# Block-sparse attention and an MLP-mixer on one Trainium2 core: the first head pair cut into row halves, a shorter gate, and a new instruction order

## The chip, the core and the metric

The kernel runs on one core of a Trainium2 chip. The core has five engines with their own in-order instruction queues: TensorE (PE in the profile; PEld is its weight load), VectorE (DVE), ScalarE (ACT), GpSimd (POOL) and SyncE (SP, which here only issues DMAs). The metric is device microseconds of one launch. The median of three runs of the kernel before is 264.33 us (264.31 to 272.79).

## What is computed

Inputs are q, k and v of shape (4, 8, 768, 64) and four MLP weights. Attention is by blocks of 64 keys: each query attends to its own block and to the three blocks with the highest gate score, all under the causal mask. A mixer follows, which mixes tokens and then channels.

```python
k_rep = k.reshape(B, H, n_blocks, block, D).mean(axis=3)
gate_scores = np.einsum('bhsd,bhnd->bhsn', q, k_rep)
gate_scores = np.where(causal, gate_scores, -1000000000.0)
top_idx = np.argsort(gate_scores, axis=-1)[..., -top_k:]
...
sel = set(top_idx[b, h, i].tolist()) | {own_block[i]}
...
scores = scale * np.matmul(q, k.transpose(0, 1, 3, 2))
mask = mask & (pos[:, None] >= pos[None, :])
attn = softmax(np.where(mask, scores, -1000000000.0))
x = np.matmul(attn, v)                          # (B, S, 512) for the mixer
...
h = np.maximum(xt @ w_tok1, 0.0) @ w_tok2
u = x + h.transpose(0, 2, 1)
h2 = np.maximum(u @ w_ch1, 0.0) @ w_ch2
return (u + h2).astype(np.float32)
```

(The softmax is written out in the reference; it is cut to one line here.)

## The kernel before

**Units of work.** The heads are taken in pairs: 4 batches of 4 pairs, 16 in all, and the 64 channels of the two heads of a pair lie on the two halves of the 128 partitions. `pair(p)` (from line 461) does one pair; `mlp(b)` (from line 693) does the channel MLP of one batch, which needs all four of its pairs.

**One pair.** k, q and v are loaded in fp32 (lines 470 to 478). For the first eight pairs ("early") k is turned by fp32 transposes on TensorE (line 486), summed over blocks of 64 by DVE (line 487), and copied to fp16 in `KA` by four copies (line 496). Later pairs have k cast to fp16 by GpSimd first (line 502), turned by six fp16 transposes (line 508) and copied by two copies (line 512); their block sums come from a separate computation per batch. q is turned in fp32 (line 519) and copied to `QT` (522), and to fp16 in `QA` (533). Twelve rows under the 64 channels of `QA` and `KA` carry the block mask: `KA` has a block indicator (`ind`, copied in line 379 ahead of everything else), `QA` a number per query and block, so that the matmul of the scores adds the mask by itself.

**The gate.** Pairs below `th` (pairs 0 to 3) use ten fp32 matmuls (line 543) of `QT` with block sums that are zero outside their own head (`ks2b`, spread by a product with `side`, line 491). The other early pairs split q and the sums into three bf16 parts (lines 499, 526, 552) and use fifteen bf16 matmuls (line 559) and three additions (564). After the causal bias (546), DVE takes the eight largest of the twelve scores (573), copies the third to PSUM (575), compares (576) and multiplies with `own`, which is 0 at a query's own block and -1 elsewhere (579). The result is turned, by TensorE (598) for pairs 0 to 4 and by DVE (584) and four small DMAs (587) from pair 5 on, and lands in `QA`.

**Scores, values, tokens.** Per head the 21 causal 128x128 tiles of scores go through three groups (`GROUPS`, line 18) of up to 1024 columns: matmuls (619), one exponential per group on ACT (626), a triangular mask on GpSimd for the diagonal tiles (634). Then 21 matmuls with v (643), the normalisation (646, 650), the token MLP (661, 665, 675, 678) and a transpose of its result (686). The channel MLP has 24 steps of four matmuls (704) with a ReLU (710, 712), and per output tile of 128 rows twelve matmuls of 512 columns (721), one addition (724) and one DMA (727).

**What sets the order.** Nothing is issued in program order. Each step is registered with `P.op(cost, function, reads, writes, priority)`. A planner (`Plan.run`, from line 114) then plays the queues forward with the given costs and picks on each engine, among what could start soon, the step with the lowest priority number. It chooses the engine too where a step names several. Priorities are the pair's time `T(p)`, set by `EARLY` and `PACE` (line 46), plus or minus a lead from the table `L` (line 47). `th` and `bd` in that table pick the kind of gate and of turning. Where TensorE would wait, matmuls of zeros are put in (line 766) until the first step of the channel MLP.

Of the kernel before, what the change touches and what calls it, by code (L numbers as in the profile page):

```python
# [17 lines left out]
GROUPS = [  # L18
# [3 lines left out]
]  # L22


def _layout():
    col, diag, width = {}, [], []
    for g, banks in enumerate(GROUPS):
        mine, w = [], 0
        for bk, pieces in enumerate(banks):
            at = 512 * bk  # L30
            for kk, q0, n in pieces:
                for i in range(n):
                    col[kk, q0 + i] = 1024 * g + at + 128 * i
# [4 lines left out]
        diag.append(mine)  # L38
        width.append(w)
    return col, diag, width  # L40


COL, DIAG, WIDTH = _layout()

EARLYP = 8
EARLY, PACE = 5.58, 13.33
L = dict(kd=28.57, qd=25.92, vd=11.57, va=-8.52, kt=12.35, kr=17.84, ke=-10.79, qt=15.5, qe=4.07, q16=14.86, g=19.74,
         b=14.78, k16=23.05, kx=14.61, kc=15.1, r=24.94, kb=35.09, ks=47.26, w1=2.86, w2=-1.57, wc1=17.92, wc2=28.28,
         tok=9.0, ml=12.54, o0=-0.3, o1=1.07, o2=2.31, o3=0.96, o4=-4.5, o5=1.61, o6=-2.0, o7=-4.89, o8=-4.68,
         o9=0.71, o10=0.86, o11=-1.11, o12=-2.65, o13=-2.86, o14=1.45, o15=0.65, m0=-2.18, m1=-0.36, m2=-0.52,  # L50
         m3=-1.94, th=3.11, bd=4.29)
# [207 lines left out]
def kernel(  # L259
# [84 lines left out]
    own1 = np.where(nidx[None, None, :] == mrow, 0.0, -1.0)  # L344
    both = np.stack([np.concatenate([a, a], axis=2)[:, 1:] for a in (gb1, own1)], axis=1).astype(np.float32)
# [8 lines left out]
    gbias, own = cst[:, 0], cst[:, 1]  # L354
# [3 lines left out]
    nc.gpsimd.memset(ind, MASKV)  # L358
# [3 lines left out]
    side = sb([128, 2, 6], FP, "side")  # L362
    nc.gpsimd.memset(side, 0.0)
    for x in range(2):
        nc.gpsimd.memset(side[64 * x:64 * x + 64, x], 1.0)
# [95 lines left out]
    def pair(p):  # L461
# [4 lines left out]
        early, thirds = p < FIRST, p >= L["th"]  # L466
        q32, k32, v32 = Buf(q32r), Buf(k32r), Buf(v32r)
        qs, ks_, vs = q[b, h:h + 2], k[b, h:h + 2], v[b, h:h + 2]
        QA, KA, VA, QT = Buf(QAr), Buf(KAr), Buf(VAr), Buf(QTr)
        for t, src, e, lead in ((k32, ks_, "SP", "kd"), (q32, qs, "ACT" if p == 0 else "SP", "qd")):  # L470
            for x in range(2):
                P.op({e: (500.0, 1600.0, 768 * 17.6 / 16)}, lambda x=x, t=t, src=src, e=e: ENG[e].dma_start(
                    out=t.t[:, :, x, :], in_=src[x].rearrange("(j p) d -> p j d", p=128)), wr=[(t, x)], pr=t0 - L[lead] - (99.0 if p == 0 else 0.0))
# [7 lines left out]
        if early:  # L481
            ks2b = kp = Buf(kppr if thirds else ksr)
            ks3 = Buf(ks3r) if thirds else None
            for i in range(2):
                t = Buf(Rr)
                P.op(pe(slow=3), lambda t=t, i=i: transposed(k32, i, t.t), rd=[(k32, 0), (k32, 1)], wr=[(t, 0)], pr=t0 - L["kt"])
                P.op(dve(HS), lambda t=t, i=i: nc.vector.tensor_reduce(
                    out=ks3.t[:, 0, 6 * i:6 * i + 6] if thirds else t.t[:, HS:HS + 6], in_=t.t[:, 0:HS].rearrange("c (n w) -> c n w", w=64),
                    axis=AX.X, op=ALU.add), rd=[(t, 0)], wr=[(ks3, i) if thirds else (t, 1)], pr=t0 - L["kr"])
                if not thirds:  # L490
                    P.op({"DVE": (150.0, 220.0)}, lambda t=t, i=i: nc.vector.tensor_tensor(
                        out=ks2b.t[:, :, 6 * i:6 * i + 6], in0=t.t[:, HS:HS + 6].rearrange("c (o n) -> c o n", o=1).broadcast_to([128, 2, 6]),
                        in1=side, op=ALU.mult), rd=[(t, 1)], wr=[(ks2b, i)], pr=t0 - L["kr"] + 0.1)
                for x in range(2):
                    def kev(e, t=t, i=i, x=x):
                        copy(ENG[e], KA.t[0:64, x, halves(i)], t.t[64 * x:64 * x + 64, 0:HS])
                    P.op({**dve(HS), **act(HS)}, kev, rd=[(t, 0)], wr=[(KA, (x, i))], pr=t0 - L["ke"])
# [312 lines left out]
```

## Time and profile before

| | |
|---|---|
| median of the runs | 264.33 us (264.31 to 272.79) |
| the profiled execution, its own time | 264.49 us |
| its span, first to last instruction | 262.8 us |
| mean granted TensorE clock | 0.998 |
| PE, DVE, ACT, POOL busy | 250.4, 157.3, 167.1, 120.0 us |
| first transposes of k / first scores / last addition start | 6.41 / 15.79 / 259.08 us |

All views show one execution. A row of the timeline or of a group names the line of the kernel, the engine, the operation and "out<-in" with the tiles' names (numbers left out), then partitions x elements and types. "x10" counts instructions. In brackets or behind the last bar stands the idle time of the engine before it, and who ended it. A busy PE is not a PE at its peak: matmuls are pipelined, and the time of one includes its latency.

### The profile page before, as it was taken

To read this page: it belongs to the slowest core of one execution; us is meant where nothing else is said; L and a number is where in the kernel's file an instruction comes from. 1 tells how busy PE (TensorE), PEld (TensorE's weight loads), DVE (VectorE), ACT (ScalarE), POOL (GpSimd) and SP (SyncE) were. 2 spreads that over 40 slices of the span, in tenths; PEclk is the share of its full clock that TensorE was granted. 3 is DMA by queue.
4 is the path that set the end of the run, shared out by engine and by line. 5 is a ranking of instruction groups with operands and counts; after the bars stand their busy time and mean duration, and the time that the engine had idled before them with its cause. 6 is when DMAs were issued, how large, how long until landed. Compare 5 with 4: busy or idle time off the path is not lost.

```text
span 262.8 us, 6757 instructions
## 1 busy us (share of the span) xinstructions
PE 250.4 (95%) x2585; PEld 172.1 (65%) x2585; DVE 157.3 (60%) x527; ACT 167.1 (64%) x265; POOL 120.0 (46%) x222
## 2 busy tenths in 40 slices
PE   7689999988999999999999999999999999999994
PEld 7566688775667677666776677657665665554541
DVE  5788997998368475786684767638574452301103
ACT  2689989975776683459974968457765661360520
POOL 8136884963256898666993807133132110000000
PEclk9999999999999999999999999999999999999999
DMA  8999997689998799943997940021002100212103
GB/s 165 224 211 215 231 221 148 102 139 146 179 269 139 190 246 220 241 85 126 213 219 158 216 114 2 8 80 42 7 2 75 54 0 2 80 40 80 44 0 120
DMA packets 88960, 33.21 MB, mean 126 GB/s; under 512 B 82464, under 2 KB 85152, under 8 KB 88736
## 3 DMA queue, kind: packets, MB, share of 16 engines
q1 hardware_dynamic: 83984, 28.33, 50.0%
q0 software_dynamic: 3232, 3.93, 9.8%
q10 hardware_dynamic: 1712, 0.52, 1.0%
q8 instruction: 20, 0.33, 0.5%
q14 instruction: 12, 0.10, 0.1%
HBM read 30.01 MB, written 6.29 MB: 138 GB/s over the span
## 4 chain that ended last, share of the span: by engine, by line
PE 83%; DVE 6%; DMA 4%; ACT 2%; issue 2%; SPq 1%; DVEq 0%; ACTq 0%
PE pm L704 20%; PE pm L721 18%; PE sc L619 12%; PE pm L643 7%; PE sc L721 5%; PE pm L419 4%; PE pm L661 4%; PE pm L675 3%; PE sc L704 3%; PE pm L559 2%; DMA k<-in_k_dram 2%; DMA QA<-bnt 2%; PE pm L686 2%; ACT E L626 1%; PE pm L508 1%
## 5 line engine op out<-in xcount | busy, mean ns | idle before, releaser
L626 ACT ACTIVATE E<-sc 128x1024 f16<-128x1024 f32 (+1 forms) x96 | 83.7, 918 | 13.8 <-PE sc L619 12.7
L634 POOL TENSOR_SCALAR_AFFINE_SELECT E<-E 128x256 f16<-128x256 f16 x96 | 38.8, 409 | 69.1 <-ACT E L626 68.6
L704 PE MATMUL pm<-uT,wc 128*128 128x384 f16 x340 | 64.3, 326 | 0.0
L721 PE MATMUL pm<-wc,h 128*128 128x512 f16 x228 | 59.2, 379 | 0.0
L704 PEld LDWEIGHTS <-wc 128*128 128x128 f16 x384 | 36.2, 98 | 23.2 <-issue 0.6
L619 PE MATMUL sc<-QA,KA 76*128 76x512 f16 (+3 forms) x256 | 49.0, 305 | 2.0 <-DMA QA<-bnt 1.1
L710 ACT ACTIVATE h<-pm 128x384 f16<-128x384 f32 x60 | 29.5, 492 | 20.9 <-PE pm L704 20.7
L721 PEld LDWEIGHTS <-h 128*128 128x128 f16 x288 | 26.6, 98 | 23.3 <-issue 1.0
L619 PEld LDWEIGHTS <-KA 76*128 76x128 f16 x256 | 22.8, 98 | 16.7 <-issue 2.9
L643 PEld LDWEIGHTS <-E 128*128 128x128 f16 x672 | 25.1, 98 | 4.9 <-issue 1.1
L643 PE MATMUL pm<-VA,E 128*128 128x65 f16 x651 | 25.5, 193 | 1.0 <-ACT uT L301 0.9
L724 DVE TENSOR_TENSOR os<-u,pm 128x512 f32<-128x512 f16 x19 | 12.9, 681 | 20.5 <-PE pm L721 19.1
L712 DVE TENSOR_SCALAR h<-pm 128x384 f16<-128x384 f32 x25 | 13.9, 555 | 13.1 <-PE pm L704 12.7
L449 POOL TENSOR_TENSOR kb<-kb 96x512 f32<-96x512 f32 (+2 forms) x18 | 20.0, 1114 | 0.0
L303 POOL CAST QA<-QT 64x768 f16<-64x768 f32 x12 | 9.8, 819 | 20.7 <-ACT QT L301 18.7
L724 DVE TENSOR_TENSOR os<-u,sc 128x512 f32<-128x512 f16 x5 | 3.3, 686 | 26.0 <-PE sc L721 26.0
L650 DVE TENSOR_TENSOR x<-pm,rc 128x384 f16<-128x384 f32 x31 | 17.2, 556 | 0.8
L678 DVE TENSOR_TENSOR u<-x,pm 128x384 f16<-128x384 f16 x30 | 15.5, 547 | 2.7 <-PE pm L675 2.5
L301 ACT COPY uT<-pm 128x384 f16<-128x384 f16 x21 | 9.1, 486 | 12.5 <-PE pm L686 12.5
L301 ACT COPY QT<-pm 128x384 f32<-128x384 f32 x24 | 11.0, 485 | 8.0 <-PE pm L419 7.8
L552 POOL TENSOR_TENSOR R<-R 128x640 bf16<-128x640 f32 x12 | 15.0, 1252 | 1.9 <-DVE R L526 0.9
L419 PE MATMUL pm<-id,q 128*128 128x128 f32 x96 | 14.6, 276 | 1.0 <-ACT QT L301 1.0
(90 smaller groups left out, 358.0 us busy)
## 6 DMA issues: line engine op xcount, KB each, us to landing
k<-in_k_dram SPq DMA_DIRECT2D x32, 192.0 KB
v<-in_v_dram SPq DMA_DIRECT2D x16, 384.0 KB
out_dram<-os SPq DMA_DIRECT2D x24, 256.0 KB
q<-in_q_dram SPq DMA_DIRECT2D x30, 192.0 KB
wc<-in_moe_w_ch_dram POOLq DMA_DIRECT2D x8, 384.0 KB, 6.3
kb<-in_k_dram SPq DMA_DIRECT2D x2, 1536.0 KB
w<-in_moe_w_tok_dram POOLq DMA_DIRECT2D x2, 384.0 KB, 6.2
QA<-bnt SPq DMA_DIRECT2D x44, 9.0 KB
```

Of the source, the lines that this page charges most:

```text
L301: e.copy(out=out, in_=in_)
L419: nc.tensor.transpose(out=t[:, 128 * j:128 * j + 128], in_=src.t[:, 3 * i + j].rearrange("p x d -> p (x d)"), identity=id32)
L449: P.op({"POOL": (step * 2.15 + 60, step * 2.15 + 140)}, lambda n=n, o=o, step=step: nc.gpsimd.tensor_tensor(out=kb.t[:, o:o + step] if n > ...
L619: nc.tensor.matmul(out=s.t[:, at:at + 128 * m], lhsT=KA.t[:, x, 128 * kk:128 * kk + 128], rhs=QA.t[:, q0:q0 + m, x, :], start=True, stop=True)
L626: nc.scalar.activation(out=E.t[:, 1024 * g_:1024 * g_ + WIDTH[g_]], in_=s.t[:, 0:WIDTH[g_]], func=AF.Exp, scale=scale)
L634: nc.gpsimd.affine_select(out=o, in_=o, pattern=[[0, 2], [1, 128]], compare_op=ALU.is_ge, fill=0.0, base=0, channel_multiplier=-1)
L643: nc.tensor.matmul(out=t[:, jq, :], lhsT=E.t[:, cc:cc + 128], rhs=VA.t[:, x, kk, :], start=(kk == 0), stop=(kk == jq))
L650: P.op(dve(384), lambda a=a, rc=rc, x=x: nc.vector.tensor_tensor(out=xp.t[:, :, 64 * x:64 * x + 64], in0=a.t[:, 0:NJ * 65].rearrange("p (j ...
L704: nc.tensor.matmul(out=m.t[:, 0:HS], lhsT=wc1[:, c, 128 * f:128 * f + 128], rhs=uT.t[:, c, HS * i:HS * i + HS], start=(c == 0), stop=(c == ...
L710: nc.scalar.activation(out=h2.t[:, f, :], in_=m.t[:, 0:HS], func=AF.Relu)
L721: nc.tensor.matmul(out=m.t, lhsT=h2.t[:, f, 128 * jj:128 * jj + 128], rhs=wc2[:, f, :], start=(f == 0), stop=(f == NFC - 1))
L724: P.op(dve(DM), lambda j=j, m=m, o=o: nc.vector.tensor_tensor(out=o.t.rearrange("p (c d) -> p c d", d=128), in0=u.t[:, :, j, :], in1=m.t.r ...
```

## The change

It has several parts, which the planner then orders anew.

1. **Pair 0 in row halves** (`CUT = 1`): its k and q come in row halves, with priorities that put the first halves first; transposes, sums, copies, gate, comparison and turning follow per half. The gate of the first half covers two of the five row tiles and six of the twelve blocks. A second layout of the score tiles, `HALVED`, puts the six tiles that need only the first halves into its first group. GpSimd may no longer make pair 0's fp16 q.
2. **Gate.** For fp32 gates the comparison reads the scores in PSUM and the third value directly; for all, it writes the mask, and two memsets on 64 partitions (GpSimd or DVE) clear each query's own block. The product with `own` is gone, and the indicator has its sign turned. Block sums always go to SBUF, and for fp32 gates two GpSimd copies spread them over the heads.
3. **k in fp16** for pairs 2 and 3 (`k0` to `k1`): GpSimd casts k, six fp16 transposes turn it, two copies fill `KA`. The fp32 transposes remain for the block sums.
4. **The last output tile** is made in two halves of 256 columns, each with its own matmuls, addition and DMA.
5. **New numbers** for nearly all priorities. `th` goes from 3.11 to 5.9, so that pairs 4 and 5 take the fp32 gate; `bd` (4.29 to 4.76) still means pair 5.

The diff, cut to its core:

```diff
+HALVED = [
+    [[(0, 1, 2), (0, 0, 1), (1, 1, 1)], [(2, 2, 1), (1, 2, 1)]],
+    [[(0, 3, 3), (5, 5, 1)], [(4, 4, 2), (1, 3, 2)]],
+    [[(2, 3, 3), (1, 5, 1)], [(3, 3, 3)]],
+]
...
-EARLY, PACE = 5.58, 13.33
-L = dict(kd=28.57, qd=25.92, vd=11.57, va=-8.52, kt=12.35, kr=17.84, ke=-10.79, qt=15.5, qe=4.07, q16=14.86, g=19.74,
...
-         m3=-1.94, th=3.11, bd=4.29)
+CUT = 1
+EARLY, PACE = 5.58, 14.57
+L = dict(kd=27.6, qd=26.51, vd=11.57, va=-8.12, kt=9.92, kr=21.45, ke=-10.79, qt=17.89, qe=-4.61, q16=15.3, g=19.76,
...
+         m2=4.07, m3=-2.96, th=5.9, bd=4.76, cu=-2.34, cs=0.51, k0=1.5, k1=3.5)
...
-    nc.gpsimd.memset(ind, MASKV)
+    nc.gpsimd.memset(ind, -MASKV)
...
-    side = sb([128, 2, 6], FP, "side")
-    nc.gpsimd.memset(side, 0.0)
-    for x in range(2):
-        nc.gpsimd.memset(side[64 * x:64 * x + 64, x], 1.0)
+    for t in ks2:
+        nc.gpsimd.memset(t, 0.0)
...
+        cut = p < CUT
+        dual = early and L["k0"] <= p < L["k1"] and not cut
+        GROUPS, COL, DIAG, WIDTH, BASE = LAYOUTS[cut]
+        parts = [(0, 2), (2, NJ - 1)] if cut else [(0, NJ - 1)]
...
+                for i in range(1 + cut):
+                    n = NJ // (1 + cut)
...
+                        out=t.t[:, n * i:n * i + n, x, :], in_=src[x, 128 * n * i:128 * n * i + 128 * n].rearrange("(j p) d -> p j d", p=128)),
+                        wr=[(t, (x, i) if cut else x)], pr=t0 - L[lead] - (99.0 - 0.2 * i if p == 0 else 0.0))
...
-                    P.op({"DVE": (150.0, 220.0)}, lambda t=t, i=i: nc.vector.tensor_tensor(
-                        out=ks2b.t[:, :, 6 * i:6 * i + 6], in0=t.t[:, HS:HS + 6].rearrange("c (o n) -> c o n", o=1).broadcast_to([128, 2, 6]),
-                        in1=side, op=ALU.mult), rd=[(t, 1)], wr=[(ks2b, i)], pr=t0 - L["kr"] + 0.1)
+                if not thirds and (cut or i == 1):
+                    def spread(z=slice(6 * i, 6 * i + 6) if cut else slice(0, NB)):
+                        for x in range(2):
+                            nc.gpsimd.tensor_copy(out=ks2b.t[64 * x:64 * x + 64, x, z], in_=ks3.t[64 * x:64 * x + 64, 0, z])
+                    P.op({"POOL": (210.0, 280.0)}, spread, rd=[(ks3, i)] if cut else [(ks3, 0), (ks3, 1)],
+                         wr=[(ks2b, i)] if cut else [(ks2b, 0), (ks2b, 1)], pr=at(i, L["kr"]) + 0.1)
+                if dual:
+                    continue
...
-        else:
+        if dual or not early:
             k16 = Buf(k16r)
...
-        P.op({"DVE": (140.0, 210.0)}, lambda: nc.vector.tensor_copy(out=third(), in_=m8.t[:, :, :, 2:3]), rd=[(m8, 0)], wr=[(g, 1)], pr=t0 - L["g"] + 0.25)
...
-            out=bn.t[:, 1:, :, 0:NB], in0=below(), in1=own.rearrange("p j (x n) -> p j x n", n=NB), op=ALU.mult),
...
+            def less(z0=z0, z1=z1, nb=nb, pair_of=pair_of):
+                u_, w_ = pair_of()
+                nc.vector.tensor_tensor(out=bn.t[:, 1 + z0:1 + z1, :, 0:nb], in0=u_, in1=w_.broadcast_to([128, z1 - z0, 2, nb]), op=ALU.is_lt)
...
+            def mine(e, z0=z0, z1=z1):
                 for x in range(2):
+                    o = bn.t[64 * x:64 * x + 64, 1 + z0:2 + z0, :, 0:1]
+                    o = bass.AP(tensor=o.tensor, offset=o.offset + 2 * (1 + z0) + x, ap=[o.ap[0], [66, z1 - z0], [32, 2]])
+                    ENG[e].memset(o, 0.0)
+            P.op({"POOL": (200.0, 270.0), "DVE": (140.0, 210.0)}, mine, rd=[(bn, i)], wr=[(bn, i)], pr=at(i, L["g"]) + 0.4)
...
+                wide = DM // 2 if b == B - 1 and j == NJ - 1 else DM
+                for w in range(0, DM, wide):
```

More of the change, by code (lines that the diff above doesn't have):

```diff
@@ L353 @@
     cstc = nc.inline_tensor(both, name="cstc").ap()
-    gbias, own = cst[:, 0], cst[:, 1]
+    gbias = cst
     nc.vector.memset(zero, 0.0)
@@ L582, in pair @@
+        bn_all = [(bn, i) for i in range(len(parts))]
         if p >= L["bd"]:
@@ L636, in pair @@
+                P.op({"POOL": (195.0 * len(DIAG[g_]), 195.0 * len(DIAG[g_]) + 50.0)}, mask, rd=[(E, g_)], wr=[(E, g_)], pr=tg + 0.2)
             a = Buf(Rr)
```

185 lines of the change are left out of this document (107 added, 78 removed).

## The prediction

> **What bounds the kernel now.** I read the page first, then the table of busy time by stretches, then the first 20 us in order of time, then the groups of instructions inside the stretch that the first two pointed to.
>
> ```profile
> span 262.8 us, 6757 instructions
> PE 250.4 (95%) x2585; PEld 172.1 (65%) x2585; DVE 157.3 (60%) x527; ACT 167.1 (64%) x265; POOL 120.0 (46%) x222
> PE   7689999988999999999999999999999999999994
> PEclk9999999999999999999999999999999999999999
> ```
>
> Over the whole span the matmul engine looks like the only bound, at full clock. The average hides two stages. The stretches (from:to, length, then busy us of each engine) part them:
>
> ```profile
> 0.00:6.40 6.40, 4.72 (x47) 4.58 (x48) 3.69 (x11) 1.49 (x2) 5.44 (x20) 1.00 0.82 162
> 6.40:15.80 9.40, 7.17 (x70) 6.46 (x71) 6.86 (x29) 6.92 (x14) 1.96 (x5) 1.00 1.20 212
> 15.80:59.00 43.20, 40.06 (x565) 32.30 (x565) 39.12 (x149) 39.41 (x59) 29.88 (x58) 1.00 1.00 181
> 59.00:64.30 5.30, 4.24 (x42) 2.67 (x41) 4.66 (x21) 2.78 (x6) 2.42 (x7) 1.00 0.98 133
> 64.30:100.00 35.70, 35.67 (x343) 23.95 (x344) 20.89 (x56) 25.93 (x39) 23.28 (x39) 1.00 0.99 205
> 100.00:150.00 50.00, 50.00 (x570) 34.66 (x569) 34.56 (x122) 33.62 (x52) 36.99 (x60) 1.00 0.89 182
> 150.00:200.00 50.00, 50.00 (x547) 34.52 (x545) 32.62 (x115) 33.95 (x54) 16.79 (x30) 1.00 0.16 45
> 200.00:259.00 59.00, 58.56 (x410) 32.91 (x408) 14.23 (x27) 23.02 (x43) 3.25 (x8) 1.00 0.12 43
> ```
>
> From 64.3 to 259 PE is busy 194.2 of 194.7 us while DVE and ACT idle a third of the time or more: there only PE work counts, and freed DVE time is worth nothing. Before 64.3 PE is idle 2.2 + 3.1 + 1.1 = 6.4 us (behind the first data), and DVE (39.12 of 43.2) and ACT (39.41) are both 91% busy between 15.8 and 59. No MLP work exists there until the first batch's four head pairs are through, so their evictions, gates and exponentials set the pace. Whatever brings that point forward brings the dense PE stretch, and the end, forward by as much, less any PE work added. The start in order of time (start, duration):
>
> ```profile
> 3.85 2.68 DVE L379 COPY KA<-ind 12x768 f16<-12x768 f16 x6 [1.72 <-POOL ind L360]
> 6.41 0.84 PE L419 MATMUL pm<-id,k 128*128 128x128 f32 x6 [0.61 <-DMA k<-in_k_dram]
> 6.96 0.96 ACT L301 CAST KA<-pm 64x384 f16<-64x384 f32 x2 [2.87 <-PE pm L419]
> 7.29 0.57 DVE L487 TENSOR_REDUCE pm<-pm 128x6 f32<-128x384 f32 x1 [0.76 <-PE pm L419]
> 15.79 0.59 PE L619 MATMUL sc<-QA,KA 76*128 76x512 f16 x3
> GB/s 0 0 0 0 0 0 0 0 0 0 0 0 81 203 213 174 133 195 210 249 285 283 293 285 285 291 286 275 221 218 221 211 224 220 217 228 227 223 248 238
> ```
>
> The data of pair 0 lands at about 6.3, and 9.4 us pass before the first scores at 15.79. The last row is the DMA rate in 40 parts of the first 6.3 us (0.1575 us each).
>
> **The change, step by step.** The profiled run took 264.49 us (span 262.8 plus 1.7 around it); the median is 264.33, so it stands 0.16 high. Terms are taken from 264.49.
>
> *(a) First loads in halves.* The same 2 x 393 KB of k and q are cut into row halves, first halves issued first on SP and on ACT. By the rate row 393 KB have moved by about 3.6 us and 786 KB by about 5.4; the data was usable at 6.3, so 0.9 after its last byte. The first halves are then usable at 4.5, 1.8 us sooner, and ACT's first eviction moves from 6.96 to some 5.1. DVE gains less: six copies of the block indicators (L379) stand ahead in its queue until 6.53, because GpSimd builds their source, and neither is changed. Its first reduction moves from 7.29 to 6.55. That is 1.85 + 0.75 = 2.6 us of two engines, 1.3 us of time. Ends: 0 (halves land together, shared with pair 1's loads) and 1.3; I take 1.1, near the upper, since issue order favours the first halves. More issues on SP (four for k instead of two, about 0.6 each by 2.56 us for four) delay pair 1's loads by 1.3 us; they were not what the engines waited for, so nothing is charged.
>
> [...]
>
> *(b) Work taken off DVE and ACT.* Groups inside 0 to 64.3 us (for the fp16 copies of k, later ones); behind the bar busy us, then mean ns. The last row gives shortest, median and longest in ns:
>
> ```profile
> L491 DVE TENSOR_TENSOR ks<-pm,side 128x12 f32<-128x12 f32 x8 | 1.2, 161 | 0.3 <-ACT KA L301 0.3
> L575 DVE COPY pm<-m 128x10 f32<-128x10 f32 x7 | 1.2, 175 | 0.0
> L579 DVE TENSOR_TENSOR bn<-pm,cst 128x120 f16<-128x120 f32 x6 | 1.7, 277 | 0.2 <-DVE rc L646 0.2
> L526 DVE TENSOR_TENSOR R<-pm,QT 128x256 f32<-128x256 f32 x3 | 1.2, 414 | 0.0
> L526 DVE TENSOR_TENSOR R<-pm,QT 128x384 f32<-128x384 f32 x3 | 1.6, 540 | 0.0
> L564 DVE TENSOR_TENSOR gm<-pm,gm 128x120 f32<-128x120 f32 x6 | 1.7, 281 | 0.1
> L303 DVE CAST KA<-pm 64x384 f16<-64x384 f32 x14 | 7.7, 552 | 0.3
> L301 ACT CAST KA<-pm 64x384 f16<-64x384 f32 x14 | 6.6, 474 | 5.1 <-PE pm L419 4.1 <-DVE KA L303 0.4 <-DVE pm L487 0.4
> L303 DVE COPY KA<-pm 64x768 f16<-64x768 f16 x11 | 6.1, 550 | 2.9 <-ACT E L626 2.1 <-PE pm L508 0.7
> L301 ACT COPY KA<-pm 64x768 f16<-64x768 f16 x5 | 4.0, 793 | 0.4 <-DVE KA L303 0.4
> L301 ACT CAST QA<-QT 64x768 f16<-64x768 f32 x7 | 5.8, 834 | 0.2
> L436 POOL COPY kpp<-ks 64x36 bf16<-64x36 bf16 x6 | 1.3, 209 | 0.3
> L365 POOL MEMSET side<- 64x6 f32 x2 | 0.5, 273 | 0.1
> L502 POOL CAST k<-k 128x768 f16<-128x768 f32 x8 | 6.5, 824 | 0.2
> L478 POOL CAST VA<-v x16: 817/826/840, 18.4 to 173.4; 128x768 f16<-128x768 f32 x16
> ```
>
> The block sums of pairs 0 to 3 are spread by two GpSimd copies instead of eight DVE multiplies: 8 x 0.161 = 1.3 off DVE. The product with `own` goes for every pair, 6 x 0.277 = 1.7 by this point. One line of the table of constants matters more than its size: `th` goes from 3.11 to 5.9, so pairs 4 and 5 leave the three-part bf16 gate for the fp32 one. With it go two subtractions each, 2 x (0.414 + 0.540) = 1.9, and two additions each, 4 x 0.281 = 1.1. The copy of the third score goes for the six pairs 0 to 5: 6 x 0.175 = 1.05. In pairs 2 and 3 eight evictions of k at a mean of 0.51 (4.1) become four of fp16, three on DVE and one on ACT as later pairs share them: 3 x 0.550 + 0.793 = 2.45, so 1.65 less. Against it pair 0 in halves pays more starts: GpSimd may no longer make its fp16 q (one copy there, one of 0.834 on ACT, become four of some 0.48 by the 64x384 row): +1.1; smaller pieces of gate and mask: an estimate of +0.6. The clears of own blocks go to GpSimd where it is free, else to DVE: +0.5. Sum 1.3 + 1.7 + 1.9 + 1.1 + 1.05 + 1.65 - 2.2 = 6.5 us of two engines, 3.2 us of time. Ends: 0, if PE or a chain of waits sets the pace, and 3.5; I take 3.2, because both engines are at 91%.
>
> GpSimd takes two copies per pair (the 64x36 row, 0.42 for both, as against 0.32 on DVE), two clears of small tiles (nearest the 64x6 memset, 0.27 each) and two casts of k (0.82 each), and loses pair 4's and 5's remainder and split. It is at 29.88 of 43.2, so this lies beside other work; what it costs if that cover is gone is the third rival.
>
> *(c) The first chain.* Two of five row tiles of the gate, then six of 21 score tiles, need only the first halves. From a reduction at 6.55: 0.57, the spread 0.42, two fifths of the fp32 gate's 1.03 below, and some 2 us (an estimate) for bias, maxima, comparison, clear, transposes and evictions; first scores near 10 instead of 15.79. In 6.4 to 15.8 DVE idles 2.5 us and ACT 2.5; exponentials that come earlier fill some of it. Ends 0 and 2.5 us of time; I take 1.2, midway, as nothing here shows the refill.
>
> *(d) PE work added.* Rows of the chain:
>
> ```profile
> 20.40 1.03 PE pm L543 x10
> 162.22 0.49 PE pm L559 x15
> 182.47 0.34 PE pm L508 x6
> ```
>
> Two fp32 gates for bf16 ones: 2 x 0.54 = 1.1. Fp16 transposes of k besides the fp32 ones, which the block sums still need: 2 x 0.34 = 0.7. Together 1.8, in the stage where PE idles 6.4 us plus fillers; but the stage also gets shorter. Ends 0 and 1.8; I take 0.9.
>
> *New order.* After 64.3 it can win no more than the 0.5 us that PE idles there to 259. What it could lose has no row; the nearest are the 6.4 us of idle PE before. MLP work is ready throughout, so I take 0.
>
> *(e) The last tile in two halves of columns.*
>
> ```profile
> 259.08 0.69 DVE L724 TENSOR_TENSOR os<-u,pm 128x512 f32<-128x512 f16 x1 [1.30 <-issue]
> GB/s 0 0 0 0 0 0 0 0 0 0 0 0 0 0 0 137 389 378 368 389 410 347 273 0 0 0 0 0 63 336 389 410 147 0 0 0 0 0 0 0
> ```
>
> The addition behind the last matmul falls from 0.69 to 0.41 (the 128x256 row above); the last transfer, five parts of 0.195 us here, halves: 0.45. Gain 0.3 to 0.7; I take 0.7. Nothing is queued behind it.
>
> Sum: 264.49 - 1.1 - 3.2 - 1.2 + 0.9 - 0.7 = 259.2 (about 259.0 for the median).
>
> **Rivals.** *Second: the freed time does not arrive.* PE is in order, and between 15.8 and 59 it shows 40.06 of 43.2, fuller than the other two. If the 1.8 us of PE work counts whole and (b) gives only a third: 264.49 - 1.1 - 1.1 - 1.2 + 1.8 - 0.7 = 262.2. That the halves land together (the change not doing what it says) gives 259.2 + 1.1 + 1.2 = 261.5 and belongs here. Against it: a pipelined matmul's latency counts as busy, so PE's real slack is larger than 3.1 us.
>
> *Third, slower: GpSimd's queue.* Spread and clear put two crossings of GpSimd into each gate, in a queue that sits on the diagonal masks, which wait for exponentials.
>
> ```profile
> POOL E L634 <- ACT E L626: 10.5, 13, 2.9
> ```
>
> That is 15 to 59 us: 13 waits, 0.81 each. Should each of the ten steps of pairs 1 to 5 stand behind one, and the lead of a pair not cover it, the gates lose 8.1 us: 264.49 - 5.3 + 8.1 = 267.3. It decides from 0.53 us a step (5.3/10). Against it: pairs are prepared ahead, and the first idle time behind a late gate is PE's, which had 3.1 us in all.
>
> [...]
>
> *Fourth: everything arrives.* (a) 1.3, (b) 3.5, (c) 2.5, (d) 0, (e) 0.7: 256.5. PE's visible slack allows it.
>
> **How the numbers follow.** First 0.48 (259.2; by itself 257.5 to 261.3), second 0.20 (262.2), third 0.14 (267.3, spread from 264.5 to 271), fourth 0.18 (256.5). The range 255.6 to 266.5 leaves out the upper half of the third and a little of the fourth, about 1 in 10 besides what was not thought of. A measurement of this kernel can tell about 2% from no change, 5.3 us: under 259.0 lie the fourth and less than half of the first, 0.39; over 269.6 a third of the third, 0.04; within, 0.57.
>
> **What would show it.** First k transposes near 4.5 to 5 us; DVE's first reduction at 6.55, right behind L379; first scores near 10. DVE's multiplies with `side` and `own` gone; two fp32 gates more. PE dense from about 59 instead of 64.3, with no idle behind it. The tail from the last matmul 0.7 shorter. The prediction is wrong if DVE or ACT falls clearly below 90% in 15 to 55 us while PE waits (second), if gates wait for GpSimd's spread or clear (third), or if PE idles after 65 us, since no term allows for the new order opening a gap there.

## The result and the profile after

The changed kernel takes 267.79 us (median of six runs, 266.29 to 269.14); the kernel before took 264.18 beside it. The ratio is 1.0138, with a 95% interval of 1.0102 to 1.0174: 3.6 us slower, where 5.3 faster was forecast. Runs of one kernel differ by the granted clock: none of the six of after had more than 0.994, while 61 of the 93 runs of before beside the experiments had 0.997 or more, so comparisons below name the clock where it matters.

The profiled run of after took 266.92 us. Its page:

```profile
span 264.9 us, 6889 instructions
PE 255.2 (96%) x2642; PEld 179.1 (68%) x2642; DVE 150.9 (57%) x513; ACT 169.3 (64%) x266; POOL 121.6 (46%) x240
PE   7799999999999999999999999999999999999993
PEclk9799999999999999999999999999999999999999
```

Over the whole span DVE lost 6.4 us of work, ACT gained 2.2 and PE 4.8, of which 2.7 are matmuls of zeros ahead of the first MLP step (8.9 us for 6.2). The clock row has a 7 in its second slice. Term (b) counts DVE and ACT up to about the first MLP step: there DVE fell from 49.68 to 46.50 us and ACT from 47.83 to 46.62, 4.4 us of two engines for the 6.5 forecast. The stretches, with the columns of the table in the prediction:

```profile
6.40:15.80 9.40, 7.52 (x78) 7.31 (x79) 5.29 (x25) 5.37 (x12) 0.96 (x6) 0.82 1.34 222
15.80:59.00 43.20, 41.99 (x588) 36.07 (x586) 36.02 (x130) 37.61 (x54) 29.11 (x67) 1.00 0.97 167
59.00:64.30 5.30, 5.19 (x49) 3.65 (x48) 3.96 (x10) 3.98 (x8) 3.59 (x7) 1.00 1.18 200
64.30:100.00 35.70, 35.70 (x359) 24.08 (x358) 21.02 (x70) 25.28 (x38) 23.38 (x39) 1.00 0.95 190
100.00:150.00 50.00, 49.45 (x548) 33.55 (x546) 33.96 (x123) 33.85 (x52) 37.99 (x62) 1.00 0.96 196
150.00:200.00 50.00, 50.00 (x565) 35.08 (x564) 32.05 (x119) 36.40 (x58) 18.34 (x32) 1.00 0.15 39
```

In 15.8 to 59 DVE fell from 39.12 to 36.02 and ACT from 39.41 to 37.61, while PE rose from 40.06 to 41.99. PE is dense from 59 on, as the prediction's list had it, and idles 0.55 us in 100 to 150, where before had none. Now the start of after in order of time:

```profile
3.86 2.96 DVE L383 COPY KA<-ind 12x768 f16<-12x768 f16 x6 [1.72 <-POOL ind L366]
4.39 0.87 PE L423 MATMUL pm<-id,k 128*128 128x128 f32 x3
4.54 0.41 ACTq L494 DMA_DIRECT2D cst<-cstc  x1
6.85 0.56 DVE L505 TENSOR_REDUCE ks<-pm 128x6 f32<-128x384 f32 x1
7.56 0.43 POOL L511 COPY ks<-ks 64x6 f32<-64x6 f32 x2 [1.77 <-DVE ks L505]
8.04 0.61 PE L576 MATMUL pm<-ks,QT 128*128 128x12 f32 x4 [2.11 <-POOL ks L511]
9.76 2.71 PE L829 MATMUL pm<-zero 128*128 128x120 f16 x28
12.65 0.75 PE L576 MATMUL pm<-ks,QT 128*128 128x24 f32 x6
13.43 0.32 DVE L580 TENSOR_TENSOR gm<-pm,cst 128x72 f32<-128x72 f32 x2 [2.32 <-PE pm L576]
16.42 0.49 PE L671 MATMUL sc<-QA,KA 76*128 76x256 f16 x5 [0.37 <-DVE QA L310]
```

The first halves are usable at 4.39 at the latest: zeros keep PE busy until about then, and it shows no wait for them. Then the lead is lost in three places. DVE holds the six indicator copies until 6.82, so the reduction runs at 6.85 and PE idles 2.11 us before the gate at 8.04. PE's queue has the next pair's transposes and 28 zeros ahead of the second half's gate (12.65). In DVE's queue both halves' bias additions stand together (x2 at 13.43), the second half's first, so the first half, whose gate was done at 8.65, waits for the second; the bias cst that they add is issued at 4.54, behind q's four transfers. The first scores come at 16.42, later than before. And the clock halves behind the idle 2.11 us (last columns: granted clock, DMA share, GB/s):

```profile
8.00:9.00 1.00, 0.96 (x7) 0.96 (x8) 0.44 (x1) 0.00 (x0) 0.00 (x0) 0.80 1.35 221
9.00:10.00 1.00, 1.00 (x8) 0.94 (x7) 0.00 (x0) 0.62 (x2) 0.00 (x0) 0.50 1.35 218
11.00:12.00 1.00, 1.00 (x13) 1.00 (x12) 0.11 (x1) 0.70 (x2) 0.37 (x2) 0.50 1.35 218
12.00:13.00 1.00, 1.00 (x15) 1.00 (x14) 0.00 (x0) 0.15 (x1) 0.00 (x0) 0.99 1.35 218
```

That is some 3.4 us at half speed (0.4 of the first row, then three whole ones). The tail:

```profile
258.96 0.49 PE L781 MATMUL sc<-wc,h 128*128 128x256 f16 x3 [0.51 <-DVE os L785]
261.46 0.41 DVE L785 TENSOR_TENSOR os<-u,sc 128x256 f32<-128x256 f16 x1
```

From the last matmul's end to the span's end it is 3.49 us (261.41 to 264.9) against 3.81 (258.99 to 262.8), but PE waited 0.51 just before.

The milestones of the profiled runs (us; "MLP" is the first step of the channel MLP):

| kernel | first k transposes | first scores | MLP | last matmul ends | span | clock |
|---|---|---|---|---|---|---|
| before | 6.41 | 15.79 | 59.01 | 258.99 | 262.8 | 0.998 |
| after | 4.39 | 16.42 | 60.65 | 261.41 | 264.9 | 0.993 |
| e2_late_ind | 4.21 | 13.60 | 57.74 | 257.88 | 261.4 | 1.000 |
| e15_first_half_by_hand | 4.38 | 11.68 | 60.83 | 262.56 | 266.1 | 0.994 |
| e17_late_less_pe | 4.42 | 14.20 | 56.96 | 258.17 | 261.7 | 1.000 |
| e18_late_less_all | 4.34 | 14.07 | 55.02 | 257.44 | 261.0 | 1.000 |

A profile shows one run. That of e2 is the shortest of its ten runs and that of e18 the second longest of its six; those of after and e15 hold a stretch at half clock, so their steps compare with the others only roughly.

### The profile page after: what moved, and what is told of

It reads as the page before. It is cut to its first block, busy times and chain, and to the rows that moved or that the text cites. A ratio compares the mean times of both kernels' runs of the same rounds, so it can differ in the third digit from the quotient of the medians.

```text
span 264.9 us, 6889 instructions
## 1 busy us (share of the span) xinstructions
PE 255.2 (96%) x2642; PEld 179.1 (68%) x2642; DVE 150.9 (57%) x513; ACT 169.3 (64%) x266; POOL 121.6 (46%) x240
## 4 chain that ended last, share of the span: by engine, by line
PE 74%; DVE 10%; POOL 7%; ACT 3%; issue 2%; SPq 1%; DMA 1%; DVEq 0%; POOLq 0%; ACTq 0%
PE pm L761 17%; PE pm L781 13%; PE sc L671 11%; PE sc L781 5%; PE pm L700 5%; PE pm L423 5%; PE pm L732 4%; POOL kb L453 3%; PE pm L718 3%; PE sc L761 3%; ACT E L683 2%; PE pm L576 2%; PE pm L594 2%; PE pm L743 2%; DVE x L707 2%
## 5 line engine op out<-in xcount | busy, mean ns | idle before, releaser
L683 ACT ACTIVATE E<-sc 128x1024 f16<-128x1024 f32 (+3 forms) x96 | 84.5, 916 | 20.6 <-PE sc L671 17.0
L691 POOL TENSOR_SCALAR_AFFINE_SELECT E<-E 128x256 f16<-128x256 f16 (+2 forms) x96 | 39.4, 413 | 58.0 <-ACT E L683 56.8
L781 PE MATMUL pm<-wc,h 128*128 128x512 f16 (+1 forms) x228 | 58.1, 373 | 0.0
L781 PEld LDWEIGHTS <-h 128*128 128x128 f16 x300 | 27.9, 98 | 23.2 <-issue 1.2
L767 ACT ACTIVATE h<-pm 128x384 f16<-128x384 f32 x57 | 28.0, 492 | 20.4 <-PE pm L761 20.3
L671 PEld LDWEIGHTS <-KA 76*128 76x128 f16 x264 | 23.9, 99 | 16.0 <-DMA QA<-bnt 0.8
L785 DVE TENSOR_TENSOR os<-u,pm 128x512 f32<-128x512 f16 (+1 forms) x19 | 12.7, 667 | 20.3 <-PE pm L781 20.3
L781 PE MATMUL sc<-wc,h 128*128 128x512 f16 (+1 forms) x72 | 18.2, 361 | 0.6 <-DVE os L785 0.5
L308 ACT CAST QA<-QT 64x768 f16<-64x768 f32 (+1 forms) x19 | 14.5, 762 | 0.7 <-DVE QT L310 0.3
L785 DVE TENSOR_TENSOR os<-u,sc 128x512 f32<-128x512 f16 (+1 forms) x6 | 3.9, 642 | 18.6 <-PE sc L781 18.6
```

What stands on the lines that cost most here:

```text
L308: e.copy(out=out, in_=in_)
L671: nc.tensor.matmul(out=s.t[:, at:at + 128 * m], lhsT=KA.t[:, x, 128 * kk:128 * kk + 128], rhs=QA.t[:, q0:q0 + m, x, :], start=True, stop=True)
L683: nc.scalar.activation(out=E.t[:, BASE[g_]:BASE[g_ + 1]], in_=s.t[:, 0:WIDTH[g_]], func=AF.Exp, scale=scale)
L691: nc.gpsimd.affine_select(out=o, in_=o, pattern=[[0, len(d)], [1, 128]], compare_op=ALU.is_ge, fill=0.0, base=0, channel_multiplier=-1)
L767: nc.scalar.activation(out=h2.t[:, f, :], in_=m.t[:, 0:HS], func=AF.Relu)
L781: nc.tensor.matmul(out=m.t[:, 0:wide], lhsT=h2.t[:, f, 128 * jj:128 * jj + 128], rhs=wc2[:, f, w:w + wide], start=(f == 0), stop=(f == NFC ...
```

## The experiments

The theory after the result: the loss lies in the first 16 us, where the first half's chain stands behind other work, and the 3.2 us of (b) cannot arrive, since PE has its own 40 of 43 us. Rivals: the half clock alone; the new order further on; GpSimd's steps in the gates (the prediction's third rival).

**e1: only the clock.**

```diff
 def gate(...):
+    if cut and z0 == 0:
+        for _ in range(34):
+            nc.tensor.matmul(out=g.t[:, 392:512], lhsT=zero, rhs=zero[:, 0:120], ...)
```

> The changed kernel with 34 matmuls of zeros ahead of the first half's gate, in the 2.1 us in which PE idled (5.9 to 8.0 us); nothing else differs, the zeros write columns that nobody reads. Theory 1 (cold clock): the idle gap is what halves the granted clock for 3.4 us or more; kept busy, PE shows a clock of 1.00 from 4 to 16 us, the mean clock is at least 0.997, the runs scatter less and the median falls from 267.8 to 265 or less. Theory 2 (PE work): the clock costs little because PE waits in that stretch anyway; the median stays within 0.7 us of 267.8. Theory 3 (order of the later work): as theory 2.

Measured 267.19 us, ratio 1.0116 [1.0093, 1.0139], at a clock of 0.997 or more in every run. First scores came at 15.01, the first MLP step at 59.23, each 1.4 sooner than in after, and further on PE lost it again:

```profile
PE sc L674 <- DMA QA<-bnt: 2.3, 2, 1.5
```

QA<-bnt are the four small transfers that bring a pair's mask into `QA`; both waits lie behind 100 us. Ahead of the longer one the mask is ready at 107.62, but SP's queue still stands at a load of v and a store of the output, and issues the first transfer at 109.51:

```profile
107.04 0.58 DVE L638 STREAM_TRANSPOSE bnt<-bn 128x384 f16<-128x384 f16 x1
109.51 3.34 SPq L641 DMA_DIRECT2D QA<-bnt  x4
```

In the profile of e2 (next), which has the same order there, the mask is ready at 106.13 and the first transfer goes at 106.16; PE has no such wait. So at full clock the kernel is no faster: the half clock is not what makes the difference in the end.

**e2: the indicator copies out of the way.** The six copies are issued behind the third, fifth and twelfth planned DVE step.

```diff
-    for t in KAr.tiles:
-        for x in range(2):
-            nc.vector.tensor_copy(out=t[64:KR, x, :], in_=ind)
...
+    n_dve, late = 0, {3: 0, 5: 1, 12: 2}
     for o in order:
+        n_dve += o.eng == "DVE"
+        if o.eng == "DVE" and n_dve - 1 in late:
+            for x in range(2):
+                nc.vector.tensor_copy(out=KAr.tiles[late[n_dve - 1]][64:KR, x, :], in_=ind)
```

> The changed kernel with the six copies of the block indicators (2.96 us of DVE, ending at 6.82) issued behind the third, fifth and twelfth of the planned DVE steps instead of ahead of all. Theory 1: the first reduction moves from 6.85 to about 5.3, the first half's gate from 8.04 to about 6.5, PE's gap shrinks below 1 us and the clock stays at 1.00; median 265 or less. If the first half still gains nothing, the first scores stay near 15 to 16 us, because the comparison of the first half stands behind that of the second in DVE's queue. Theory 2: first scores move but the median stays within 0.7 us of 267.8.

Measured 264.58 (ten runs), ratio 1.0002 [0.9976, 1.0029]: beside the kernel before, the loss is gone. The reduction and the gate of e2:

```profile
4.77 0.56 DVE L502 TENSOR_REDUCE ks<-pm 128x6 f32<-128x384 f32 x1 [2.63 <-PE pm L420]
5.96 0.61 PE L573 MATMUL pm<-ks,QT 128*128 128x12 f32 x4 [0.49 <-POOL ks L508]
13.60 0.49 PE L668 MATMUL sc<-QA,KA 76*128 76x256 f16 x5 [0.51 <-DVE QA L310]
```

The medians mix clocks: e2's six runs at 1.000 took 263.35 to 264.83 (median 264.1), its four at 0.987 to 0.994 took 266.30 to 267.88, no less than after at such clocks (266.29 to 269.14). e1 keeps the clock apart, since it is after, with zeros added, at full clock: its median is 3.1 us above that of e2 at full clock. So the head of DVE's queue costs some 3.1 us. 1.5 of them are there at the first MLP step (59.23 against 57.74); the rest comes behind it, where e1 has the waits for QA<-bnt. What is left of the change is worth nothing that shows.

**e4 and e6: parts alone, planned anew.** e4 sets `CUT = 0`; e6 keeps after's code with the numbers of before (`th=3.11`, `PACE` 13.33, no early fp16 k, no halves).

> The changed kernel with pair 0 whole again (CUT = 0), all else as changed, planned anew. Theory 1: the cold clock came with the halves, so the clock is 0.997 or more and the time 266 or less. Theory 2 (1.8 us more PE work and nothing to show for it): 266 to 268, with first scores near 16 as before. Theory 3: the numbers were found for the halves and fit the whole pair badly: over 268.

> The new gate, the spread and the clears on GpSimd and the last tile in two halves, but the old numbers of the order (th 3.11, PACE 13.33), pair 0 whole and no early pair with k in fp16, planned anew. PE work is that of the kernel before. Theory 1 and theory 2: no cold clock and no added PE work, so the time is at or a little under the kernel before, 262.5 to 264.3 (the tail gives 0.3 to 0.7). Theory 3 (any new plan loses a few us on chip that the planner does not see, and GpSimd's part of the gate is late): 265 or more.

Measured 268.67 (ratio 1.0167 [1.0141, 1.0194]) and 267.57 (1.012 [1.0091, 1.015]). Neither isolates its part: each has another order throughout. e4 took that time at 0.994 to 1.000. All four runs of e6 had 0.981 to 0.987, so its loss cannot be parted into order and clock.

**e7 and e8: e2 with PE kept busy ahead of the first gate, then with more PE work.** e7 adds 14 zeros ahead of e2's first gate; e8 also seven zeros to each gate of the pairs 1 to 5.

> The changed kernel with the indicator copies moved back as before and 14 matmuls of zeros ahead of the first half's gate. A control with the clock held up: 0.999 or more in every run, and 263.4 to 264.5 with little scatter, if the longer runs of the kernel with late indicator copies (those at a clock of 0.994 and less) come from the cold clock alone.

> The control with 35 matmuls of zeros more (seven ahead of each gate of pairs 1 to 5, some 1.8 us of PE). If PE sets the pace between the first scores and the first MLP step (theory 2, now the favoured one), that stage grows from 44.1 to between 45 and 46 and the run by 1 to 1.8 us. If DVE and ACT set it, as the prediction had it, both stay within 0.5 us of the control.

Measured 266.28 (1.0057 [1.0025, 1.0089]) and 268.29 (1.0131 [1.0077, 1.0185]). The steady clock that e7 expected did not come: in its profile the clock is at half from about 15.4 to 22.2 us, behind gaps of PE of at most 0.51 us between 12 and 15. Runs at 0.997 or more: 264.35 to 265.21 for e7 (three), 266.43 and 267.12 for e8. Some 1.8 us of zeros cost 1.7 between the medians of these few runs.

**e9 and e10: the prices in the kernel before, order kept.** e9 lets twelve fp16 k copies of the pairs 3 to 5 write 16 columns of 384 (it leaves out most of these pairs' fp16 k); e10 puts 35 zeros into the gates of the pairs 1 to 5.

```diff
-    copy(ENG[e], KA.t[0:64, x, halves(i)], t.t[64 * x:64 * x + 64, 0:HS])
+    n = 16 if 3 <= p <= 5 else HS
+    copy(ENG[e], KA.t[0:64, x, HS * i:HS * i + n], t.t[64 * x:64 * x + 64, 0:n])
```

> The kernel before, with twelve copies of k to fp16 (pairs 3 to 5) shrunk from 384 to 16 columns, in the same order: most of those pairs' fp16 k is left out, and some 4.5 us of DVE and ACT time with it; PE work is the same. As the prediction argued (DVE and ACT at 91% set the pace, freed time counts by half), the first MLP step moves 2 us or more forward and the run is 262.3 or less. Under theory 2 the step moves by 0.7 us at most, and the run stays above 263.5.

> The kernel before with 35 matmuls of zeros (seven ahead of each gate of pairs 1 to 5, some 1.8 us of PE), in the same order. Under theory 2 it is 1 to 1.8 us slower, 265.3 to 266.1. If PE has slack before 59 us, as term (d) of the prediction took for half of it, 264.3 to 265.2.

Measured 264.05 (0.9993 [0.9979, 1.0007]) and 266.72 (1.0094 [1.0064, 1.0125]). The stage from the first scores to the first MLP step, in e9 and then in e10:

```profile
15.63:58.30 42.67, 39.76 (x565) 32.30 (x565) 36.42 (x149) 38.50 (x59) 29.42 (x58) 1.00 1.03 184
```

```profile
16.89:60.69 43.80, 41.24 (x594) 33.52 (x594) 38.98 (x149) 39.38 (x58) 29.88 (x58) 1.00 0.97 173
```

In e9 DVE had 2.7 us and ACT 0.9 less in the stage than in before (39.14 and 39.43). Its median does not move, but at full clock (0.997 or more, six and fifteen runs) it is 263.73 against 264.31, and the first MLP step comes 0.7 sooner: 0.6 us for 3.6 freed, a sixth, where the prediction counted half. In e10 the one run at full clock took 265.68, 1.4 more than that median of before, for some 1.8 us of zeros; the three others ran at 0.991 to 0.994. The stage itself grew by 0.6 only (43.22 to 43.80): seven of the zeros stand ahead of the first scores, and so does a stretch at half clock in this profile.

**e11 and e12: e2 with less PE work, e2 with cst issued first, both planned anew.** e11 sets `th=3.11, k0=9.5, k1=9.5`; e12 changes the priority of cst from -99 to -200.

> The kernel with the six constant copies of KA moved behind planned DVE steps (e2_late_ind: 264.58, its fast runs at full clock 263.35 to 264.83), with th back at 3.11 and no pair's k in fp16 (k0 = k1 = 9.5), planned anew. It takes from TensorE what term (d) of the prediction counted (1.8 us of busy time) and gives VectorE and ScalarE back the k copies of two pairs and the gate steps of two. If TensorE's work in order sets the pace behind the first scores, the first scores stay near 13.6, the stage from there to the first MLP step falls from 44.1 to about 42.7, and the time falls by 1 to 2 us, to 262.6 to 263.6. If VectorE and ScalarE set it, as the prediction had it, the time rises by half of the returned work, 1 to 2 us, to about 266. If the order that the planner finds decides more than either, the time moves outside both and the difference shows as waits of TensorE and not as busy time.

> e2_late_ind with one number more: the causal bias cst is due first, so that ScalarE's queue issues it ahead of the four transfers of q, as before (priority -200 instead of -99), planned anew. If what is left of the first chain's delay is the order that the late cst forces on VectorE (both halves' bias additions together, the second half's first), the first scores come at 10.5 to 11.5 instead of 13.6. If TensorE's work alone then sets the end, the time falls by as much, to 262 to 262.5. The rival, after e1_warm: the gain at the start comes back as waits for loads or for the chain of masks further on (there 2.3 us for QA<-bnt), and the time stays within 1 us of 264.6.

Measured 267.25 (1.0111 [1.0077, 1.0146]) and 270.39 (1.0171 [1.0117, 1.0224]); at a clock of 1.0, e12 took 267.53 and 267.86. e12's first scores came earlier (12.43), its end 3 us or more later. At full clock the medians are 3.0 and 3.6 us above e2's. Again a new order outweighs its cause: of e11's three readings only the last, that the order decides, is left (in its stage PE is idle 3.4 us, in e2 0.9, but is also busy 3.2 us longer), and both of e12's failed.

**e14: the last block whole.** `wide = DM` on e2, planned anew.

> e2_late_ind with the last block of the last MLP step written whole again (wide = DM), planned anew. In e2_late_ind the last block's first matmul starts at 254.43 and the span ends at 261.4, 6.97 later; in the kernel before 256.24 and 262.8, 6.56 later. The prediction gave the halves a gain of 0.7: then this kernel takes 0.7 more than e2_late_ind, about 265.3, with the stretch from that matmul to the end at 7.7. By the rows of e2_late_ind the halves cost 0.4 (24 matmuls and a wait of 0.51 for os, against 0.3 won behind the last matmul): then the stretch is near 6.6 and the time 0.2 to 0.6 less.

Measured 264.71 (1.0009 [0.9983, 1.0034]) against e2's 264.58. The halves are worth nothing that shows, for or against.

**e15: the first half's lead, by hand.** On e2's order, steps of the first half are moved ahead and nothing else; the diff moves ten of them.

```diff
+    for ns, before in [((9,), 1), ((42, 45, 46, 47), 17), ((51,), 37), ((52, 53), 96), ((57,), 98), ((58,), 100)]:
+        moved = [next(o for o in order if o.n == n) for n in ns]
+        order = [o for o in order if o not in moved]
+        i = next(i for i, o in enumerate(order) if o.n == before)
+        order[i:i] = moved
```

> e2_late_ind (264.58; first scores at 13.6, first MLP step at 57.74) with its order kept, and of the first pair's first half alone eleven steps moved ahead by hand: the causal bias cst is issued behind the first halves of q, the half's bias addition, search, comparison and clear stand ahead of the second half's transposes, its mask transposes and copies ahead of the second pair's, its scores and exponentials right behind the second half's gate. No planner runs anew, so nothing else moves. If the first half's lead was lost to its place in the queues, the first scores come at 9 to 10.5. If TensorE then only has its own work left, the stage from there to the first MLP step grows by less than it starts earlier, and the time falls to 262 to 263.5. The rival: the first half's scores are 0.5 us of TensorE and the rest waits for the second half and for the next pairs' loads as before, so that the first MLP step stays at 57.5 to 58 and the time at 264.6, within 0.7.

Measured 266.24 (1.0036 [1.0013, 1.006]); at 0.997 or more, five of six runs took 264.78 to 264.90, against 263.35 to 264.83 for e2. The first scores came at 11.68, not quite in the range expected, and brought nothing: the rival, a time within 0.7 of 264.6, held at full clock, although in this profile, at half clock from 17.0 to 20.4, the first MLP step came at 60.83. PE now waits behind the moved steps, for their evictions (10.71) and for the second half's (15.31):

```profile
10.71 0.55 PE L420 MATMUL pm<-id,k 128*128 128x128 f32 x3 [0.67 <-DVE QA L310]
15.31 1.29 PE L573 MATMUL pm<-ks,QT 128*128 128x24 f32 x10 [0.50 <-ACT QA L308]
```

**e16 to e19: which engine sets the pace behind the first scores.** Order and waits are kept. e16 and e17 replace four of five fp32 gate matmuls of a pair (the profile shows these five as ten) by small fp16 ones of zeros, in before (pairs 1 to 3) and in e2 (pairs 1 to 5); e19 relieves ACT and DVE in e2; e18 does both. They leave out gate scores (e16, e17, e18), and parts of the exponentials and of k (e18, e19; k is cut as in e9). The two edits:

```diff
+    lhsT, rhs = (zero, zero[:, 0:2 * nb]) if 1 <= p <= 5 and j else (QT.t[...], ks2b.t[:, :, 0:nb])
...
+    n = WIDTH[g_] - (256 if 3 <= p <= 5 else 0)
+    nc.scalar.activation(out=E.t[:, BASE[g_]:BASE[g_] + n], in_=s.t[:, 0:n], func=AF.Exp, scale=scale)
```

> The kernel before, with four of the five gate matmuls (fp32, 24 columns, about 0.12 us each in a row) of the pairs 1 to 3 replaced by fp16 matmuls of zeros into the same columns; the first of each five stays, so that every wait stays. It leaves out four fifths of these pairs' gate scores. Twelve matmuls, some 1.0 us of TensorE's time less in the stage between the first scores and the first MLP step, VectorE and ScalarE as they were. If TensorE's work in order is the bound there, the time falls by 0.8 to 1.2, to about 263.4, and the stage from 43.2 to about 42.2. If VectorE and ScalarE set the pace, as the prediction had it, it stays within 0.3 of the kernel before.

> e2_late_ind (264.58) with the same done to the pairs 1 to 5, which there all have fp32 gates: twenty matmuls, some 1.7 us of TensorE's time less, order and waits as they were; four fifths of these pairs' gate scores are left out. If the work that the change adds to TensorE is what eats the earlier start, the time falls by 1.4 to 2, to 262.6 to 263.2, under the kernel before, and the first MLP step comes near 56.1. If what eats it lies elsewhere (waits for loads, the order behind the first MLP step), the time stays within 0.7 of 264.58.

> e17_late_less_pe (264.54; TensorE's 2 us of gate work gone, but TensorE then waited 1.5 us for ScalarE's exponentials) with less for the other two as well, order and waits kept: the 18 exponentials of the pairs 3 to 5 leave out their last 256 columns (18 times about 0.21 us of ScalarE, 3.8 us), and the eight fp16 k copies of the pairs 4 and 5 write 16 columns of 384 (8 times about 0.37, 3 us of VectorE and ScalarE). It leaves out these parts of the softmax and of k, beside the gate scores. If TensorE, VectorE and ScalarE are bound together, so that relief of one only moves the wait, relief of all three comes off the time: 262 to 263, the first MLP step near 55.5. If the stream of loads sets the pace, the time stays at 264.5, within 0.7, with waits of TensorE for transfers in place of those for ScalarE.

> e2_late_ind with ScalarE's and VectorE's relief of e18_late_less_all alone (18 exponentials 256 columns narrower, eight k copies of 16 columns), TensorE's work whole. If ScalarE's exponentials set the pace, the time falls by 1.5 to 2, to about 262.8. If it takes TensorE's relief as well, or if the loads set it, it stays within 0.7 of 264.58.

| kernel | relieved | median | ratio to before | runs at 0.997 or more |
|---|---|---|---|---|
| e16 | PE, in before | 265.99 | 0.9995 [0.9943, 1.0047] | 263.52, 263.81 |
| e2 | nothing | 264.58 | 1.0002 [0.9976, 1.0029] | 263.35 to 264.83 |
| e17 | PE | 264.54 | 0.998 [0.9938, 1.0022] | 262.93 to 265.10 |
| e19 | ACT, DVE | 265.10 | 1.0004 [0.9976, 1.0033] | 263.31 to 265.32 |
| e18 | PE, ACT, DVE | 261.86 | 0.9895 [0.9873, 0.9918] | 261.49 to 262.76 |

The stage of e2, of e17 and of e18:

```profile
13.60:57.74 44.14, 43.20 (x600) 37.20 (x600) 36.99 (x133) 38.12 (x54) 29.24 (x67) 1.00 1.04 182
```

```profile
14.20:56.96 42.76, 39.77 (x580) 33.20 (x580) 37.31 (x133) 37.87 (x54) 29.12 (x67) 1.00 1.01 185
PE sc L668 <- ACT E L680: 1.5, 3, 1.1
```

```profile
14.07:55.02 40.95, 39.28 (x581) 33.10 (x580) 34.35 (x133) 35.21 (x54) 29.00 (x67) 1.00 1.08 194
PE sc L669 <- DMA QA<-bnt: 1.8, 3, 1.0
```

The rows of waits count the whole run. The three profiles above are at full clock, and there the medians are 264.1 (e2), 264.5 (e17), 263.4 (e19) and 261.86 (e18, all six runs).

PE's relief alone (e17) brings nothing to the time. PE waits 1.5 us for exponentials in its stage, in e2 0.2. The stage still becomes shorter, and the first MLP step comes 0.8 sooner, but PE then takes 201.21 us to its last matmul, in e2 200.14. Relief of ACT and DVE alone (e19; 4.9 us of both in the stage) brings at most 0.7. Relief of all three brings 2.3, more than the two together. So PE and the pair of ACT and DVE are bound together there, and each hides most of the other's relief, while most of the work added on PE shows (e8, e10). In the kernel before, PE's relief (e16, an estimated 1.0 us) brought 0.7 (263.67 against 264.39), but in two runs only; the other four had 0.973 to 0.987.

e18 shows a further bound. Its first MLP step comes 2.7 us sooner than e2's, but its 1.8 us of waits for QA<-bnt all stand behind that step, between 60 and 230 us, so part of the gain is lost there.

## Why the prediction was wrong, step by step

*(a)* held in part: first halves usable at 4.39 at the latest for 4.5 predicted, ACT's first eviction at 5.65 for 5.1, the reduction at 6.85 for 6.55, right behind the indicator copies, as the prediction had it. The 1.1 us did not arrive, because what follows did not use them. The prediction had the copies ahead of the reduction and took them only as a smaller gain; what waits behind them it put at nothing. e1 beside e2 puts that at some 3.1 us, the largest single piece of the miss, and delaying the copies was what the change lacked.

*(b)* is the step that failed first: "both engines are at 91%", so that half of their freed time counts. The stage from the first scores to the first MLP step, before and then after:

```profile
15.79:59.01 43.22, 40.08 (x565) 32.31 (x565) 39.14 (x149) 39.43 (x59) 29.89 (x58) 1.00 1.00 181
```

```profile
16.42:60.65 44.23, 43.28 (x601) 37.19 (x601) 37.05 (x133) 38.47 (x55) 29.28 (x67) 1.00 0.98 169
```

It grew by 1.0 us although DVE and ACT had less to do. Less was freed (4.4 us for 6.5), and it counted for less: e9 has a sixth in place of half. e17, e18 and e19 show why: PE stood at 93% beside the two already in the kernel before (40.08 of 43.22). The second rival named it ("PE is in order, ... fuller than the other two") and gave (b) a third, 1.1 us; a sixth of 4.4 is 0.7. Its 262.2 failed by its other terms.

*(c)* failed in place and in kind. First scores near 10 became 16.42, through the three places above, of which the prediction saw only the first. And even first scores at 11.68 (e15) bring nothing: the six early tiles are 0.5 us of PE, and by e17 to e19 the pace behind them is set by three engines together.

*(d)* was mis-sized. Half of the added PE work was taken as hidden, but e8 and e10 show most of it (1.7 and 1.4 of some 1.8 us), and there was a little more of it. The gate and k between first scores and first MLP step, before and then after:

```profile
L543 PE MATMUL pm<-ks,QT 128*128 128x24 f32 x22 | 2.8, 264 | 0.0
L559 PE MATMUL pm<-kpp,R 128*128 128x72 bf16 x20 | 1.2, 197 | 0.0
L559 PE MATMUL pm<-kpp,QT 128*128 128x72 bf16 x10 | 1.2, 197 | 0.0
L419 PE MATMUL pm<-id,k 128*128 128x128 f32 x24 | 3.9, 283 | 0.4 <-DVE R L526 0.4
```

```profile
L576 PE MATMUL pm<-ks,QT 128*128 128x24 f32 x50 | 6.2, 266 | 0.0
L530 PE MATMUL pm<-id,k 128*128 128x128 f16 x12 | 1.0, 219 | 0.0
L423 PE MATMUL pm<-id,k 128*128 128x128 f32 x30 | 4.8, 274 | 0.0
```

The two rows of L559 overlap in time: the bf16 gates of pairs 4 and 5 run from 34.56 to 35.20 and from 49.29 to 49.94, 1.3 us together. A fp32 gate takes 1.24 (6.2 for five). So the two that were exchanged add 1.2 us for the 1.1 forecast, and the fp16 k 1.0 for 0.7: 2.2 for 1.8. PE's busy time in that stage grew by 3.2 (40.08 to 43.28), because work also moved in from ahead of the first scores: most of pair 1's gate, six fp32 transposes of k (0.9) and some zeros (1.2 for 0.4). So the change traded DVE time for PE time in a stage where both were full.

*(e)* 0.3 of the 0.7 came behind the last matmul, and the 0.51 wait for an output buffer ahead of it took it back; e14 shows nothing either way.

*New order at 0* was 0.8 us off behind the first MLP step of after (200.76 us to the last matmul, 199.98 before), and not safe in general: planned anew, e11 and e12 stand 3.0 and 3.6 us above e2 at full clock. (That ACT idles a third of the time or more behind 64.3 was read a little high: it is 27% in 64.3 to 100. No term uses it.)

*The third rival* was right in sign and wrong in place. GpSimd's own steps are short (0.43 at 7.56), and PE waited for them once (2.11 us, most of it for the late reduction), in the gates of later pairs hardly. That its price of 267.3 is near the measurement is luck: the cause was a queue's head, on DVE.

An estimate from these prices: 2.3 us of (a) and (c) and 0.7 of (e) that did not come, 2.5 missing from (b), 1.3 more for (d) and 3.1 for the queue's head make 9.9, where 8.6 lie between 259.2 and 267.79. The pieces are not independent, and their prices come from different kernels.

What stays open lies behind the first MLP step. From there to its last matmul PE takes 200.1 us in the profile of e2, 200.8 in after, 201.2 in e17, 202.4 in e18, 202.7 in e1 and 203.3 in e7, all with one order there; the waits for QA<-bnt are, in this order, 0, 0.3, 0.6, 1.8, 2.3 and 2.4. So these waits make most of the difference, and in these profiles they take back much of what an earlier first MLP step wins. The prediction took 0 for this stretch. Why SP's queue issues these transfers late (seen in e1) was not taken apart, nor which steps of a new order cost e11 and e12 their time.

## What to carry to other kernels

When two or three engines are nearly full in the same stage (here 91, 91 and 93%), freed time on some of them is worth little until the others are relieved too (a sixth in e9, nothing in e17): price such a step by the engine that it loads, not by the one that it frees. An earlier first transfer is worth only as much as the queues behind it are cleared: look at what stands at the head of each queue at the new time, and move that in the same change. Compare runs at one granted clock, since a median can mix two (e2's ten runs: 1.000 and 0.987 to 0.994). Where a planner makes the order, compare parts by edits that keep the order; a new plan moves several us by itself.

## What the runs showed of the hardware

In the profiles of after, e15, e7 and e12 PE's granted clock falls from 1.00 to 0.50 and comes back: in after for some 3.4 us (8.6 to 12.0), in e15 for some 3.4 (17.0 to 20.4), in e7 for some 6.8 (15.4 to 22.2), in e12 for some 10.2 (13.4 to 23.7). In after it falls behind 2.11 us without a matmul. In e7 gaps of at most 0.51 us (between 12 and 15) came ahead of it, in e15 gaps of 0.37 and 0.50 (between 14 and 16, where PE was busy 0.45 and 0.69 us of one each):

```profile
16.00:17.00 1.00, 1.00 (x12) 0.92 (x12) 0.28 (x1) 0.66 (x1) 1.00 (x3) 1.00 1.28 216
17.00:18.00 1.00, 1.00 (x7) 0.77 (x6) 0.97 (x11) 0.92 (x1) 1.00 (x2) 0.51 1.28 215
```

There PE was busy in the microsecond before the fall and during it. Runs of before at a lower mean clock are about 1 us longer: beside the experiments the span's median is 262.6 (262.0 to 263.7) in 61 runs at 0.997 or more, and 263.6 (262.7 to 264.7) in 28 runs at 0.990 to 0.994. Runs of one kernel come at either clock (e2: six at 1.000, four at 0.987 to 0.994), so what sets it off in a single run stays open, and 14 zeros ahead of one gate did not prevent it (e7, 0.987 in its profile).

Matmuls overlap in time: the 22 of L543 above are 2.8 us busy at a mean of 264 ns each, 5.8 us one by one.
